# One core, GFNet filter and gated FFN: DRAM scratch stored by sides, filters copied inside SBUF, a new order of the first weight loads, filler matmuls from a built-in constant

## The chip, the core and the metric

The kernel runs on one core of a Trainium2 chip. The core has five engines with instruction queues of their own: TensorE (PE; its weight loads are shown as PEld), VectorE (DVE), ScalarE (ACT), GpSimd (POOL) and SyncE (SP), which here issues every DMA. Each engine runs its queue in order; semaphores tie the queues together. TensorE writes to PSUM, from which DVE and ACT read; all else lives in SBUF with its 128 partitions, or in DRAM. Sixteen DMA engines move the data. The metric is the device time of one launch in microseconds (us), as the median of several runs.

## The reference

```python
x = A_x                                   # [1, 2048, 640] bf16
xn = _layernorm(x, axis=-1)
X = rfft2(xn); X = X * (A_w_r + 1j * A_w_i); s = irfft2(X)     # filter [2048, 321], bf16
g = silu((gelu(xn @ w_gate) * (xn @ w_up)) @ w_down)           # 640 -> 1536 -> 640
return x + s * g
```

A spectral filter (a 2-D real Fourier transform over 2048 rows and 640 columns, a product with a complex filter, and the way back) and a gated feed-forward network read the same normalised input; their product is added to `x`.

## The kernel before

**Slabs.** Row n of `x` is written as n = 16 n2 + n1. `X` holds it as [128 partitions (n2), 16 slabs (n1), 640]. A slab is normalised by `stats` (two `half_stats` of 320 columns on DVE, L174, and their aggregate, L179), `root` (DVE adds the epsilon, POOL raises to the power -1/2, L190) and `norm` (DVE, L196), or by `norm_act` on ACT.

**FFN.** Four slabs make a group g of 512 columns. `slab_T` transposes a normalised slab into `xnT[g]`, on TensorE with the identity or by a DMA transpose; `slab_Tparts` does it for slabs 0 and 1 in two parts (L773, L774). `ffn_piece(g, t, k, c0, c1_)` makes one tile t of 128 of the 1536 hidden units, for gate (k = 0, `Wg`) or up (k = 1, `Wu`), on the columns c0 to c1_: five matmuls over 640 inputs (L714). The gate goes through Gelu on ACT into `ge`, three buffers (L718); the up half is multiplied by it on DVE into `uT` (L720). PSUM has two banks each for gate and up (`psA`, tags g and u), so an up piece needs the DVE product of the up piece two before it. `down_third` does the third matmul (L738), with Silu or Tanh (L743, L746, L747).

**The start.** Group 0 can't wait for four slabs. `ffn_slab(j, tk)` makes pieces of 128 columns for slab j alone. The first three entries of the list `back` do this for slabs 0 and 1 and tiles 0 to 2, with the statistics and norms of slabs 1 to 3 between them; `GG` and `REST` name the pieces. Then come pieces of 256 columns: tiles 3 to 7 on the first half of the group (h0), tiles 0 to 7 on the second (h1). All the rest of group 0 and groups 1 to 3 use 512 columns.

**Filler matmuls.** `warm_pe(n)` issues n matmuls of 256 columns whose result nobody reads (L520): 19 at the very start and two after slab 0's transposes. Both operands are `ones`, which DVE sets by a memset (L202).

**Filter.** The transforms are matmuls with matrices made in the kernel: `slab_S1` (L484) over n2, `group_D` over the columns for a group of one or three slabs (`d_group`, L494 and L498), evacuated by ACT or DVE into `zd` (L510). Then 16 slabs must be combined, for which data must cross partitions: `group_D` stores `zd` to the DRAM scratch `ZDR` (L512), and `load_B2` reads it back as `B2` with another partition meaning (L530). `s2_in` multiplies with `MG` (L556), copies on ACT (L564) and multiplies with both filters `W1` and `W2` on DVE (L568); `s2_out` goes back with `N1`, `N2` (L583), copies on ACT (L589) and stores to `UDR` (L592). This runs in eleven bursts, two for three of 16 filter rows each and one for the last row. `load_V` reads `UDR` as `V` (L603); `gather` (L613), `slab_S1i` (L631), `group_Di`, `group_cs` and `group_Y` do the way back, and `finish` multiplies with the FFN's result, adds `x` and stores.

**Filters in SBUF.** `w_rows` loads `A_w_r` into `W1` and `A_w_i` into `W2`. Partition p = 64 hh + 4 k1 + 2 ri + pm holds rows for k1 with sign pm; both ri hold the same. Each call loads 16 partitions (every fourth) for both `lo`, 16 rows of 321 each, in reverse order for pm = 1 (L118, L120, L121, L123). Rows are padded to LP = 322 elements. `w_edge` halves the first and the last column on POOL (L127).

**Order.** The program is written in order by hand: `back` is the list of FFN steps, and `put(s, ...)` hangs other work behind step s. Each engine's queue follows that order. Every DMA of the kernel stands in SP's one queue, and the DMAs use eight completion semaphores in turn, so a DMA also waits until the one eight places before it has landed.

Of the kernel before, what the change touches and what calls it, by code (L numbers as in the profile page):

```python
# [14 lines left out]
P = 128  # L15
S = 2048
D = 640
L = 321
# [13 lines left out]
def kernel(  # L32
# [28 lines left out]
    ZDR = dram.tile([2, NS, P, L], BF16)  # L61
    UDR = dram.tile([2, NS, P, L], BF16)
# [6 lines left out]
    W1 = wts.tile([P, 2, NS, LP], BF16)  # L69
    W2 = wts.tile([P, 2, NS, LP], BF16)  # L70
# [6 lines left out]
def build(nc, env):  # L77
# [17 lines left out]
    load_w(0, 0, 3)  # L95
    load_x(1, 1)
    load_w(1, 0, 1)
    load_w(1, 1, 3)
    load_x(2, 2)
    load_gu(3, 5)  # L100
    load_gu(5, 7)
    load_gu(7, 8)
# [9 lines left out]
    def w_rows(i, hh, ri, pm):  # L112
        WT, sp = spw[i]
        p0 = hh * 64 + ri * 2 + pm
        for lo in range(2):
            u0 = lo * 32 + hh * 16
            if pm == 0:
                nc.sync.dma_start(out=WT[p0:p0 + 61:4, lo, :, 0:L], in_=sp[:, u0:u0 + 16, :])  # L118
            elif u0 == 0:
                nc.sync.dma_start(out=WT[p0:p0 + 61:4, lo, 1:NS, 0:L], in_=sp[:, 127:112:-1, :])  # L120
                nc.sync.dma_start(out=WT[p0:p0 + 61:4, lo, 0, 0:L], in_=sp[:, 64, :])  # L121
            else:
                nc.sync.dma_start(out=WT[p0:p0 + 61:4, lo, :, 0:L], in_=sp[:, 128 - u0:112 - u0:-1, :])  # L123
# [77 lines left out]
    ones = gtile([256], BF16)  # L201
    nc.vector.memset(ones, 1.0)  # L202
# [30 lines left out]
    def affine(name, src, a, b):  # L233
# [4 lines left out]
    u_f, hi_f, s_f, h_f, pf, n1_f, z_f = bits(  # L238
        "pb", [(0, 63), (6, 1), (0, 31), (5, 1), (0, 127), (1, 15), (0, 1)])
# [14 lines left out]
    u64 = fma("u64", e64, 64.0, u_f)  # L254
# [48 lines left out]
    root(0, 1)  # L303
    inv_consts()
# [199 lines left out]
    def group_D(i):  # L504
        n0, n = DF[i]
        pd = d_group([Zt.pop(n0 + a) for a in range(n)], FT, LH)
        zd = zdbuf[:, i % 2, 0:n]
        for b in range(2):
            ev = nc.vector.tensor_copy if i in (2, 5) and b == 1 else nc.scalar.copy
            ev(out=zd.rearrange("p a c (m b) -> p a c m b", b=2)[:, :, :, :, b], in_=pd[b])  # L510
        for a in range(n):
            nc.sync.dma_start(out=ZDR[:, n0 + a].rearrange("c p l -> p c l"), in_=zd[:, a, :, 0:L])  # L512

    warm_bank = []

    def warm_pe(n):
        if not warm_bank:
            warm_bank.append(bank(0))
        for _ in range(n):
            nc.tensor.matmul(warm_bank[0][:, 0:256], lhsT=ones[:, 0:P], rhs=ones, start=True, stop=True)  # L520
# [3 lines left out]
    def load_B2():  # L524
        B2 = big.tile([P, NH, L], BF16, tag="sB", name="B2")
        zv = ZDR.rearrange("c n (z a k h) l -> a (c n z) k h l", z=2, a=2, k=2)
# [43 lines left out]

    uv = UDR.rearrange("c n (z a k h) l -> a (c n z) k h l", z=2, a=2, k=2)

    def s2_out(b):
# [16 lines left out]
        if l0 + w == L:  # L590
            for lo in range(2):
                nc.sync.dma_start(out=uv[lo][:, :, h0:h0 + n, :], in_=us[64 * lo:64 * lo + 64, :, :, :])  # L592
# [162 lines left out]
    GG, REST = ((0, 0), (1, 0)), ((0, 1), (2, 0))  # L755
# [39 lines left out]
    def put(s, *item):  # L795
        plan[s].append(item)
# [70 lines left out]
    for k in range(16):  # L867
        put(8 + k if k < 8 else (32, 35, 38, 41, 44, 44, 47, 47)[k - 8], w_rows, k // 8, k % 8 // 4, k % 2, k % 4 // 2)
# [32 lines left out]
    warm_pe(19)  # L901
# [44 lines left out]
```

## Time and profile before

| | |
|---|---|
| median of 3 runs | 204.1 us (203.77 to 204.25) |
| profiled execution | 204.42 us, of it 202.6 us from first to last instruction (the span) |
| granted TensorE clock | 1.000 |
| chain that ended last | PE 90%, DVE 4%, DMA 2%, issue 1%, POOL 1% |
| DMA | 31.77 MB in 43315 packets; 41504 of them under 2 KB |
| PE busy by fortieths of the span | 7899999999999999999999999999999999999993 |
| DMA busy by fortieths of the span | 5999999899799999729995233569501334224211 |

A digit is the busy share of one fortieth (5.1 us) in tenths, 9 for 90% or more. "Busy" of PE counts a matmul from its start to its modelled end, and matmuls overlap, so a stretch of nines is not proof of full rate. In rows of the DMA view, the last number is the time from the issue on SP to the landing.

Times of single transfers are from the same execution. The loads at the start, with their issue and landing:

| transfer | KB | issued | landed |
|---|---|---|---|
| X slab 0 | 160 | 0.72 | 3.06 |
| Wg tiles 0-2 | 480 | 1.16 | 5.48 |
| X slab 1 | 160 | 1.63 | 5.99 |
| Wu tile 0 | 160 | 2.19 | 6.69 |
| Wu tiles 1-2 | 320 | 2.66 | 7.80 |
| X slabs 2-3 | 320 | 3.23 | 8.65 |
| Wg tiles 3-4 | 320 | 4.06 | 9.80 |
| Wu tiles 3-4 | 320 | 4.54 | 10.93 |

And around the scratch: the last three stores to `ZDR` were issued at 83.81, 84.21 and 84.72 and landed at 86.74, 88.07 and 88.92. The ten loads of `B2` were issued from 89.00 on, 0.65 apart; the first four landed at 92.72, 93.91, 95.03 and 96.20. The last store to `UDR` landed at 131.97; the loads of `V` were issued from 132.10 on and the first five landed at 134.48, 135.17, 136.15, 138.13 and 139.12. The first copy of `gather` ran at 136.45, the one for slabs 2 and 3 at 138.28.

### The profile page before, as it was taken

Reading aid. Unit: us, or ns where it says so; the run is one execution under the profiler, and the core shown is the slowest. Engines: PE = TensorE matmul, PEld = TensorE weight load, DVE = VectorE, ACT = ScalarE, POOL = GpSimd, SP = SyncE. Lnnn points to the kernel's source line nnn. Section 1 sums busy time; section 2 is a strip of 40 time slices with the busy share of each in tenths; the row PEclk is TensorE's granted clock in tenths of the full one; section 3 lists DMA queues with packets and bytes.
Section 4 is the critical chain, followed back from the end, with each engine's and each line's share of the span. In section 5 each row is a group of like instructions: output and inputs, shape, how many; then the busy total and the mean of one; then the engine's idle time right before and its main releaser. Section 6 shows DMA issues by size and latency. Waiting matters only on the chain.

```text
span 202.6 us, 4209 instructions
## 1 busy us (share of the span) xinstructions
PE 195.6 (97%) x1574; PEld 119.8 (59%) x1589; DVE 129.3 (64%) x340; ACT 122.4 (60%) x208; POOL 33.4 (16%) x61
## 2 busy tenths in 40 slices
PE   7899999999999999999999999999999999999993
PEld 5688854777555555566644333457775555556762
DVE  7886966786488982533576465342358776867672
ACT  2448657857886768423788688425375647476631
POOL 5327779953000200100000000000000000000000
PEclk9999999999999999999999999999999999999999
DMA  5999999899799999729995233569501334224211
GB/s 167 306 297 305 372 310 142 158 147 137 153 170 143 173 174 174 180 43 226 213 228 111 44 97 101 130 164 317 172 0 68 97 102 127 69 92 144 86 69 60
DMA packets 43315, 31.77 MB, mean 157 GB/s; under 512 B 12192, under 2 KB 41504, under 8 KB 43296
## 3 DMA queue, kind: packets, MB, share of 16 engines
q1 hardware_dynamic: 43296, 31.52, 71.4%
q8 instruction: 12, 0.20, 0.4%
q14 instruction: 7, 0.06, 0.1%
HBM read 21.66 MB, written 7.88 MB: 146 GB/s over the span
## 4 chain that ended last, share of the span: by engine, by line
PE 90%; DVE 4%; DMA 2%; issue 1%; POOL 1%; SPq 0%; ACT 0%; DVEq 0%
PE psu L714 25%; PE psg L714 24%; PE psg L738 13%; PE psu L738 12%; PE pd L494 5%; PE pz L484 2%; PE pv L631 2%; PE pu L583 2%; DMA X<-in_A_x_dram 2%; PE px L556 2%; PE pd L498 2%; DVE st L174 1%; DVE uT L720 1%; POOL rst L190 1%; PE pt L326 0%
## 5 line engine op out<-in xcount | busy, mean ns | idle before, releaser
L714 PE MATMUL psu<-xnT,Wu 128*128 128x512 bf16 (+2 forms) x289 | 60.9, 339 | 0.6 <-issue 0.2
L714 PE MATMUL psg<-xnT,Wg 128*128 128x512 bf16 (+2 forms) x286 | 60.4, 338 | 0.9 <-issue 0.5
L720 DVE TENSOR_TENSOR uT<-psu,ge 128x512 bf16<-128x512 f32 (+2 forms) x59 | 34.3, 585 | 29.8 <-PE psu L714 22.5
L718 ACT ACTIVATE ge<-psg 128x512 bf16<-128x512 f32 (+2 forms) x59 | 30.5, 518 | 27.6 <-PE psg L714 25.9
L738 PEld LDWEIGHTS <-uT 128*128 128x128 bf16 x384 | 36.3, 98 | 14.6 <-issue 0.6
L714 PEld LDWEIGHTS <-Wu 128*128 128x128 bf16 x295 | 26.6, 98 | 22.9 <-issue 2.7
L714 PEld LDWEIGHTS <-Wg 128*128 128x128 bf16 x295 | 26.6, 98 | 21.9 <-issue 1.5
L738 PE MATMUL psg<-Wd,uT 128*128 128x320 bf16 (+1 forms) x192 | 30.3, 302 | 0.0
L738 PE MATMUL psu<-Wd,uT 128*128 128x320 bf16 (+1 forms) x192 | 29.2, 296 | 0.0
L568 DVE TENSOR_TENSOR X<-xs,W 128x972 bf16<-128x972 bf16 (+2 forms) x22 | 13.3, 646 | 10.6 <-ACT xs L564 10.6
L174 DVE BATCH_NORM_STATS2 st<-X 128x6 f32<-128x320 bf16 x32 | 14.2, 482 | 0.5 <-DMA X<-in_A_x_dram 0.3
L633 ACT CAST W<-pv 128x640 bf16<-128x640 f32 x16 | 11.1, 692 | 5.4 <-PE pv L631 5.4
L510 ACT CAST GEN<-pd 128x966 bf16<-128x966 f32 (+1 forms) x10 | 10.4, 1102 | 5.3 <-PE pd L498 5.3
L656 ACT ACTIVATE W<-pd 128x960 bf16<-128x960 f32 (+2 forms) x14 | 10.1, 780 | 5.0 <-PE pd L498 5.0
L486 ACT CAST GEN<-pz 128x640 bf16<-128x640 f32 x16 | 11.0, 697 | 3.2 <-PE pz L484 3.2
L589 ACT CAST X<-pu 128x486 bf16<-128x486 f32 (+4 forms) x22 | 12.3, 558 | 0.3
L564 ACT CAST xs<-px 128x972 bf16<-128x972 f32 (+2 forms) x11 | 10.3, 936 | 2.4 <-PE px L556 2.4
L190 POOL TENSOR_TENSOR rst<-ve,mhalf 128x1 f32<-128x1 f32 (+2 forms) x9 | 6.5, 717 | 29.5 <-DVE ve L188 29.5
L662 DVE TENSOR_TENSOR W<-W 128x960 bf16<-128x960 bf16 (+1 forms) x12 | 6.8, 599 | 4.8 <-ACT W L656 4.8
L689 DVE TENSOR_TENSOR Yall<-Yall,G 128x640 bf16<-128x640 bf16 (+3 forms) x18 | 8.1, 450 | 2.1 <-ACT G L743 1.9
L747 DVE SCALAR_TENSOR_TENSOR G<-th,psu 128x320 bf16<-128x320 f32 x8 | 3.9, 488 | 8.4 <-ACT th L746 8.4
L452 DVE TENSOR_TENSOR f<-uvt 128x512 bf16<-128x512 bf16 x16 | 6.7, 421 | 3.0 <-PE pz L484 2.9
(137 smaller groups left out, 202.5 us busy)
## 6 DMA issues: line engine op xcount, KB each, us to landing
ZDR<-GEN SPq DMA_DIRECT2D x16, 160.5 KB, 5.3
xt<-in_A_x_dram SPq DMA_DIRECT2D x8, 320.0 KB, 3.5
UDR<-X SPq DMA_DIRECT2D x10, 240.8 KB, 3.6
W<-in_A_w_r_dram SPq DMA_DIRECT2D x14, 160.5 KB, 7.7
W<-in_A_w_i_dram SPq DMA_DIRECT2D x14, 160.5 KB, 6.0
out_dram<-Yall SPq DMA_DIRECT2D x14, 160.0 KB, 1.8
B<-ZDR SPq DMA_DIRECT2D x8, 240.8 KB, 5.5
Vin<-UDR SPq DMA_DIRECT2D x6, 321.0 KB, 6.3
```

What stands on the lines that cost most here:

```text
L174: nc.vector.bn_stats(out=st[:, k, :], in_=X[:, n1, 320 * k:320 * k + 320])
L486: nc.scalar.copy(out=Zt[n1], in_=pz)
L494: nc.tensor.matmul(out[a][g], lhsT=lhs[a][:, g, :], rhs=T[:, g, 0:w], start=(a == 0), stop=False)
L510: ev(out=zd.rearrange("p a c (m b) -> p a c m b", b=2)[:, :, :, :, b], in_=pd[b])
L564: nc.scalar.copy(out=xs, in_=px[:, :, 0:n * w].rearrange("p k (h l) -> p k h l", l=w))
L568: nc.vector.tensor_tensor(out=pp[-1], in0=xs, in1=WT[:, :, h0:h0 + n, l0:l0 + w], op=ALU.mult)
L589: nc.scalar.copy(out=us[:, :, :, c0:c0 + (w + 1 - m) // 2], in_=pv[:, :, :, m:w:2])
L633: nc.scalar.copy(out=vs, in_=pv)
L714: nc.tensor.matmul(ps, lhsT=WT[:, c, t * P:(t + 1) * P], rhs=xnT[g][:, c, c0:c1_], start=(c == 0), stop=(c == 4))
L718: nc.scalar.activation(out=ges[t], in_=ps, func=ACT.Gelu_apprx_tanh)
L720: nc.vector.tensor_tensor(out=uT[g][:, t, c0:c1_], in0=ps, in1=ges[t], op=ALU.mult)
L738: nc.tensor.matmul(ph, lhsT=uT[g][:, t, j * P:(j + 1) * P], rhs=Wd[:, t, c0:c1_], start=(t == 0), stop=(t == NT - 1))
```

## The change

Four things change.

1. *Scratch by sides.* `ZDR` and `UDR` get an outer axis a, the parity of the partition that wrote (or will read) the row, and the row index within a side runs to 64. The constant `u64` from which `Tinv` and `Tfwd` are made changes with it, so that the same numbers come out at the permuted partitions. `group_D` stores from every second partition: four stores per group of three slabs (two for the single slab) instead of one per slab. `load_B2` and the `UDR` stores now move all 128 partitions for one half of the filter rows (hh), where they moved 64 partitions for both; their number and bytes stay. `load_V` has 20 loads into every second partition instead of 10 into all.
2. *Filters copied in SBUF.* Only the partitions with ri = 0 are loaded from DRAM, nine loads for each filter instead of 18; those with pm = 0 in runs of 16 rows at once, for which the padding of the rows goes (L for LP). `w_twin` then copies them to ri = 1 from SBUF to SBUF, two copies for each filter.
3. *Start.* The first gate load has tiles 0 and 1, and all loads now have two tiles. Slabs 0 and 1 alone are used on tiles 0 to 3 instead of 0 to 2, in the order gate, gate, up, up; the pieces of 256 columns on h0 begin at tile 4. An empty step keeps the numbering of the later steps.
4. *Filler matmuls.* `ones` becomes a constant that the framework sets on POOL ahead of the program; 20 filler matmuls instead of 19 stand first in PE's queue, and two more, whose moving operand is a copy of slab 0's variance, behind them.

```diff
-    ZDR = dram.tile([2, NS, P, L], BF16)
-    UDR = dram.tile([2, NS, P, L], BF16)
+    ZDR = dram.tile([2, 2, NS, 64, L], BF16)
+    UDR = dram.tile([2, 2, NS, 64, L], BF16)
...
-    W1 = wts.tile([P, 2, NS, LP], BF16)
-    W2 = wts.tile([P, 2, NS, LP], BF16)
+    W1 = wts.tile([P, 2, NS, L], BF16)
+    W2 = wts.tile([P, 2, NS, L], BF16)
...
     load_x(0, 1)
-    load_w(0, 0, 3)
+    load_w(0, 0, 2)
     load_x(1, 1)
-    load_w(1, 0, 1)
-    load_w(1, 1, 3)
+    load_w(1, 0, 2)
+    load_gu(2, 4)
     load_x(2, 2)
-    load_gu(3, 5)
-    load_gu(5, 7)
-    load_gu(7, 8)
+    load_gu(4, 6)
+    load_gu(6, 8)
     load_x(4, 4)
...
+    def w_plus(i, hh, lo):
+        WT, sp = spw[i]
+        p0 = hh * 64
+        u0 = lo * 32 + hh * 16
+        nc.sync.dma_start(out=WT[p0:p0 + 61:4, lo].rearrange("p h l -> p (h l)"),
+                          in_=sp[:, u0:u0 + NS, :].rearrange("k h l -> k (h l)"))
+
+    def w_minus(i, hh, lo):
+        WT, sp = spw[i]
+        p0 = hh * 64 + 1
+        u0 = lo * 32 + hh * 16
+        if u0 == 0:
+            nc.sync.dma_start(out=WT[p0:p0 + 61:4, lo, 1:NS, :], in_=sp[:, 127:112:-1, :])
+            nc.sync.dma_start(out=WT[p0:p0 + 61:4, lo, 0, :], in_=sp[:, 64, :])
+        else:
+            nc.sync.dma_start(out=WT[p0:p0 + 61:4, lo, :, :], in_=sp[:, 128 - u0:112 - u0:-1, :])
+
+    def w_twin(i, pm):
+        v = spw[i][0].rearrange("p a h l -> p (a h l)")
+        nc.sync.dma_start(out=v[2 + pm:P:4], in_=v[pm:P:4])
...
-    ones = gtile([256], BF16)
-    nc.vector.memset(ones, 1.0)
+    ones = nc.const_aps.tensor(1.0, (P, 256), BF16)
+    warm_bank = []
+
+    def warm_pe(n, rhs=ones):
...
+            nc.tensor.matmul(warm_bank[0][:, 0:256], lhsT=ones[:, 0:P], rhs=rhs, start=True, stop=True)
+
+    warm_pe(20)
...
-    u64 = fma("u64", e64, 64.0, u_f)
+    u64 = fma("u64", e64, 64.0, fma("u_f", z_f, 32.0, kh_f))
...
     root(0, 1)
+    wv = consts.tile([P, 1], BF16, name="wv")
+    nc.vector.tensor_copy(out=wv, in_=mva[0][:, 0, 1:2])
+    warm_pe(2, wv.to_broadcast([P, 256]))
     inv_consts()
...
-        for a in range(n):
-            nc.sync.dma_start(out=ZDR[:, n0 + a].rearrange("c p l -> p c l"), in_=zd[:, a, :, 0:L])
+        for a in range(2):
+            if n == 1:
+                nc.sync.dma_start(out=ZDR[a, :, n0].rearrange("c p l -> p c l"), in_=zd[a:P:2, 0, :, 0:L])
+            else:
+                for c in range(2):
+                    nc.sync.dma_start(out=ZDR[a, c, n0:n0 + n].rearrange("n p l -> p n l"),
+                                      in_=zd[a:P:2, :, c, 0:L])
...
-            for lo in range(2):
-                nc.sync.dma_start(out=B4[64 * lo:64 * lo + 64, :, h0:h1, :], in_=zv[lo][:, :, h0:h1, :])
+            for hh in range(2):
+                nc.sync.dma_start(out=B4[:, hh, h0:h1, :], in_=zv[:, hh, h0:h1, :])
...
-            for lo in range(2):
-                nc.sync.dma_start(out=uv[lo][:, :, h0:h0 + n, :], in_=us[64 * lo:64 * lo + 64, :, :, :])
+            for hh in range(2):
+                nc.sync.dma_start(out=uv[:, hh, h0:h0 + n, :], in_=us[:, hh, :, :])
...
             for c in range(2):
-                nc.sync.dma_start(out=V[:, n0:n0 + n, c * L:c * L + L],
-                                  in_=UDR[c].rearrange("n p l -> p n l")[:, n0:n0 + n, :])
+                for a in range(2):
+                    nc.sync.dma_start(out=V[a:P:2, n0:n0 + n, c * L:c * L + L],
+                                      in_=UDR[a, c, n0:n0 + n].rearrange("n p l -> p n l"))
...
-    GG, REST = ((0, 0), (1, 0)), ((0, 1), (2, 0))
+    Q = [((t, 0), (t + 1, 0), (t, 1), (t + 1, 1)) for t in (0, 2)]
...
-    back = [(run, (ffn_slab, 0, GG), (norm_parts, 1), (vt_iota, 1), (ffn_slab, 0, REST), (slab_Tparts, 1),
-             (ffn_slab, 0, ((1, 1), (2, 1))),
-             (half_stats, 2, 0)),
-            (run, (ffn_slab, 1, GG + REST[:1]), (half_stats, 2, 1), (root, 2, 1), (ffn_slab, 1, REST[1:])),
-            (run, (ffn_slab, 1, ((1, 1), (2, 1))), (norm, 2), (stats, 3), (root, 3, 1))]
+    back = [(run, (ffn_slab, 0, Q[0]), (norm_parts, 1), (vt_iota, 1), (ffn_slab, 0, Q[1][0:2]), (slab_Tparts, 1),
+             (ffn_slab, 0, Q[1][2:4]), (half_stats, 2, 0)),
+            (run, (ffn_slab, 1, Q[0][0:3]), (half_stats, 2, 1), (root, 2, 1), (ffn_slab, 1, Q[0][3:4] + Q[1][0:1])),
+            (run, (ffn_slab, 1, Q[1][1:4]), (norm, 2), (stats, 3), (root, 3, 1))]
     for h in range(2):
-        for t in range(0 if h else 3, NP):
+        for t in range(0 if h else 4, NP):
             back.append((ffn_part, 0, t, h))
+    back.insert(3, (run,))
...
-    for k in range(16):
-        put(8 + k if k < 8 else (32, 35, 38, 41, 44, 44, 47, 47)[k - 8], w_rows, k // 8, k % 8 // 4, k % 2, k % 4 // 2)
+    WL = [(hh, lo) for lo in range(2) for hh in range(2)]
+    for i, places in enumerate(((8, 9, 10, 11, 12, 13, 14, 15, 26, 27), (32, 32, 35, 35, 38, 38, 41, 41, 47, 48))):
+        for k in range(4):
+            put(places[2 * k], w_minus, i, *WL[k])
+            put(places[2 * k + 1], w_plus, i, *WL[k ^ 1])
+        for pm in range(2):
+            put(places[8 + pm], w_twin, i, pm)
...
-    warm_pe(19)
     norm_parts(0)
```

More of the change, by code (lines that the diff above doesn't have):

```diff
@@ L110, in build @@
     spw = [(WT, src.rearrange("(k1 r) l -> k1 r l", k1=NS)) for WT, src in ((W1, A_w_r), (W2, A_w_i))]
-    def w_rows(i, hh, ri, pm):
+    def w_plus(i, hh, lo):
         WT, sp = spw[i]
-        p0 = hh * 64 + ri * 2 + pm
-        for lo in range(2):
[L116 to L123, printed above, removed]
+        p0 = hh * 64
[14 more added lines that the diff above has]
+        nc.sync.dma_start(out=v[2 + pm:P:4], in_=v[pm:P:4])
     def w_edge(i):
@@ L199, in norm @@
             done.add(("n", n1))
-    ones = gtile([256], BF16)
-    nc.vector.memset(ones, 1.0)
+    ones = nc.const_aps.tensor(1.0, (P, 256), BF16)
+    warm_bank = []
+    def warm_pe(n, rhs=ones):
+        if not warm_bank:
+            warm_bank.append(psA.tile([P, 512], FP32, tag="g", name="psg"))
+        for _ in range(n):
+            nc.tensor.matmul(warm_bank[0][:, 0:256], lhsT=ones[:, 0:P], rhs=rhs, start=True, stop=True)
+    warm_pe(20)
     negpi = c1("negpi")
@@ L236, in affine @@
         return t
-    u_f, hi_f, s_f, h_f, pf, n1_f, z_f = bits(
-        "pb", [(0, 63), (6, 1), (0, 31), (5, 1), (0, 127), (1, 15), (0, 1)])
+    kh_f, hi_f, s_f, h_f, pf, n1_f, z_f = bits(
+        "pb", [(1, 31), (6, 1), (0, 31), (5, 1), (0, 127), (1, 15), (0, 1)])
     cs_f = h_f
@@ L510, in group_D @@
             ev(out=zd.rearrange("p a c (m b) -> p a c m b", b=2)[:, :, :, :, b], in_=pd[b])
-        for a in range(n):
-            nc.sync.dma_start(out=ZDR[:, n0 + a].rearrange("c p l -> p c l"), in_=zd[:, a, :, 0:L])
[L514 to L520, printed above, removed]
+        for a in range(2):
[5 more added lines that the diff above has]
+                                      in_=zd[a:P:2, :, c, 0:L])
     st_b = {}
@@ L525, in load_B2 @@
         B2 = big.tile([P, NH, L], BF16, tag="sB", name="B2")
-        zv = ZDR.rearrange("c n (z a k h) l -> a (c n z) k h l", z=2, a=2, k=2)
+        zv = ZDR.rearrange("a c n (z k h) l -> (a c n z) k h l", z=2, k=2)
         B4 = B2.rearrange("p (k h) l -> p k h l", k=2)
         for h0, h1 in ((0, 3), (3, 6), (6, 9), (9, 12), (12, 16)):
-            for lo in range(2):
-                nc.sync.dma_start(out=B4[64 * lo:64 * lo + 64, :, h0:h1, :], in_=zv[lo][:, :, h0:h1, :])
+            for hh in range(2):
+                nc.sync.dma_start(out=B4[:, hh, h0:h1, :], in_=zv[:, hh, h0:h1, :])
         st_b["B2"] = B2
@@ L569, in s2_in @@
         st_b[b] = pp
-    uv = UDR.rearrange("c n (z a k h) l -> a (c n z) k h l", z=2, a=2, k=2)
+    uv = UDR.rearrange("a c n (z k h) l -> (a c n z) k h l", z=2, k=2)
     def s2_out(b):
@@ L590, in s2_out @@
         if l0 + w == L:
-            for lo in range(2):
-                nc.sync.dma_start(out=uv[lo][:, :, h0:h0 + n, :], in_=us[64 * lo:64 * lo + 64, :, :, :])
+            for hh in range(2):
+                nc.sync.dma_start(out=uv[:, hh, h0:h0 + n, :], in_=us[:, hh, :, :])
     st_c = {}
```

## The prediction

> **What bounds the kernel.** I read the page's busy shares first, then sums by stretch, then the chain of waits at the start, and last the rows of the places that the change touches.
>
> ```profile
> PE 195.6 (97%) x1574; PEld 119.8 (59%) x1589; DVE 129.3 (64%) x340; ACT 122.4 (60%) x208; POOL 33.4 (16%) x61
> ```
>
> ```profile
> 0.00:5.00 5.00, 3.83 (x19) 2.70 (x19) 3.86 (x40) 1.49 (x2) 2.55 (x10) 1.00 0.54 165
> 5.00:15.00 10.00, 8.90 (x106) 7.21 (x105) 8.28 (x32) 4.86 (x14) 2.73 (x5) 1.00 1.17 303
> 15.00:94.00 79.00, 78.42 (x642) 51.00 (x646) 52.40 (x139) 51.61 (x84) 28.16 (x47) 1.00 1.01 188
> 94.00:132.00 38.00, 37.68 (x283) 17.16 (x287) 21.91 (x37) 28.00 (x48) 0.00 (x0) 1.00 0.65 136
> ```
>
> Columns of the second view: stretch, its length, then busy us of PE, PEld, DVE, ACT, POOL, granted clock, DMA share, GB/s. From 15 us on TensorE is busy without a break that matters; a change that removes no matmul can gain only before 15 us, or where PE waits for the scratch in DRAM. The same DMA engines are full up to 94 us, but nothing waits for them there. The chain at the start (start us, us, what):
>
> ```profile
> 1.63 4.36 DMA X<-in_A_x_dram
> ...
> 6.01 0.90 DVE st L174 x2
> ...
> 7.41 0.58 POOL rst L190
> ...
> 8.01 0.39 DVE X L196
> ...
> 8.45 0.56 PE pt L773 x5
> ...
> 12.73 0.81 DVE st L174 x2
> ...
> 13.89 0.44 DVE uT L720
> ...
> 14.37 0.71 PE psu L714 x5
> ```
>
> PE runs out of slab 0's pieces at 7.66 (last start 7.60) and stands 0.79 us until slab 1 is normalised; it stands 0.23 at 11.89 and 0.30 at 14.37, both for a PSUM bank that DVE (L720) has still to read. That is 1.32 us between the first gate matmul (6.44) and full work. Full work needs 0.056 us per 128-column matmul (five to a piece: 0.28) and 0.109 per 256-column one.
>
> The scratch: PE's second half of the first filter burst, and the load that it waits for.
>
> ```profile
> 93.95 0.10 PEld L556 LDWEIGHTS <-MG 64*64 64x64 bf16 x1 [0.30 <-issue]
> B<-ZDR SPq DMA_DIRECT2D x1, 240.8 KB, 4.2
> ```
>
> The second line is the second B load alone: issued at 89.69, landed 4.2 us later, at 93.91. PE could have gone on at about 93.72, so this wait is worth 0.23 us.
>
> **The sum, step by step.** All in the profiled execution's time (span 202.6, 204.42 in all); the median of the runs is 204.1, so I take the difference off the median.
>
> *Filler matmuls.* The 19 start at 1.17, behind DVE's memset of `ones` (0.27 us, L202), 0.21 us each. Afterwards they need no memset and can start near 0.75, when the other engines do (ACT at 0.72); 20 end at about 5.0 and two more, which wait for a DVE copy behind slab 0's variance (about 4.45), at about 5.45. The transposes behind them on PE start at 5.53 in any case: DVE's norm is ready then. Gain 0; loss 0.1 if the copy, 0.06 us of DVE time, pushes the norm at 5.09 (DVE is idle 0.15 before it, which covers it). DVE loses the memset and gains one small operation; X's slab 0 lands at 3.06 and sets the rest. The 256-column filler costs 0.21 up to 4.99 and 0.11 from 5.91, so PE's slow state ends between; starting earlier can only help this, by an amount no row shows: 0 taken, 0.2 as bound.
>
> *Load order.* Landings follow each other by the time that each takes: 1.13 us per 320 KB of gate or up tiles (9.80 to 10.93), 0.51 per 160 KB of X, 1.44 for 480 KB (3 x 128 columns: 640 packets of 768 bytes, 40 per DMA engine, at the 36 ns that the trace gives one). So Wg 0-1 lands at 5.48 - 1.44 + 1.13 = 5.17, X slab 1 at 5.68 (5.99 before), Wu 0-1 at 6.81, Wg 2-3 at 7.94, Wu 2-3 at 9.07, X slabs 2-3 at 9.92 (8.65 before).
>
> *Slab 0 on four tiles.* First gate at 6.44 as before; four pieces end at 7.66 as before. Pieces g2, g3 wait for Wg 2-3: 7.97 to 8.53, 0.31 lost. DVE: slab 1's stats start at 5.73, when the norm of slab 0 is done, 0.28 earlier; but the two products u0, u1 (0.29 each) now stand ahead of slab 1's norm in its queue. Stats, root and constants end at 7.63, the products at 8.2, so the norm starts 0.16 later than the 8.01 of before and the transposes come at about 8.6 (0.05 lost). They end at 8.95; u2, u3 wait for Wu 2-3 until 9.10. Slab 1 starts at 9.66 against 9.39, with two more pieces (0.56) done: 0.29 ahead. Then the third wait: u3 of slab 1 needs the bank of u1, whose product stands behind X 2-3's half statistics (0.49, 0.21, 0.15 on DVE); I get 0.59 there against 0.23, and none where 14.37 was, because four 256-column pieces (2.2 us) now cover slab 3's statistics (1.25). Lost in all: about 0.31 + 0.05 + 0.05 + 0.59 = 1.0 against 1.32. Gain 0.3. Bounds: all waits gone, 1.3; weights 0.5 us later than this, 0.25 lost. The piece count and columns are the same otherwise; ACT and DVE have two more small operations each (0.28), on queues with room.
>
> *Filters.* Each of W1, W2: 18 loads before, now 9 loads and two SBUF copies of 642 KB. The old 160 KB loads landed 1.1 us apart. W1 had landed at 48.9, was scaled on POOL at 50.3, and nothing stands behind that there until 65.4; W2 landed at 83.4, and both are first used at 95.4. Cover of 12 us or more; the copies must wait for their loads and stand in SP's queue ahead of ZDR stores and transposes, whose data come later (49.9, 76.9). Cost 0. If a copy took 10 us, ZDR's last group (83.8) would sit behind it.
>
> *W's row pitch* goes from 322 to 321, so every other row starts off a 4-byte word. Rows:
>
> ```profile
> L720 DVE TENSOR_TENSOR uT<-psu,ge 128x256 bf16<-128x256 f32 x6 | 2.4, 416 | 1.6 <-PE psu L714 0.8 <-ACT ge L718 0.8
> L720 DVE TENSOR_TENSOR uT<-psu,ge 128x128 bf16<-128x128 f32 x6 | 1.6, 288 | 0.1
> L568 DVE TENSOR_TENSOR X<-xs,W 128x972 bf16<-128x972 bf16 x8 | 5.0, 662 | 4.7 <-ACT xs L564 4.7
> L568 DVE TENSOR_TENSOR X<-xs,W 128x642 bf16<-128x642 bf16 x2 | 0.9, 496 | 0.9 <-ACT xs L564 0.9
> L613 DVE COPY vr<-Vin x10: 185/221/222, 136.5 to 172.0; 128x256 bf16<-128x256 bf16 x6, 128x128 bf16<-128x128 bf16 x4
> ```
>
> L720 reads float32: (416 - 288) / 128 = 1.0 ns per element. L568: (662 - 496) / 330 = 0.50, two at a time. If the odd pitch took that away, 972 elements would take about 0.49 us more, twice per burst. The nearest row is L613: its first copy of a pair reads runs that start at element 289, its second at even places, and both forms show one duration (221, 222 at 256 elements). So 0 taken. The Trainium skill, Advanced Engine Details and Errata, section "VectorE Performance Modes", asks for a start on 4 bytes in this mode; by it the total would be that of the second rival. The Trainium skill's Vector Engine (DVE) Microarchitecture Reference, section 5.1, says that alignment made no difference when measured, and by that it stays at the sum below; L613 agrees with the latter, though with one source only.
>
> *Scratch by sides.* The last ZDR group goes out in four stores instead of three: same packets, one issue more (0.45 to 0.5). In the trace's packet records its data is through by 86.9 and the last landing is at 88.92: the landing is not set by the issue. I take the same 5.1 us from data to landing, and 0.5 more as bound. B's loads of 240.8 KB land 1.16 us apart while they fill 64 partitions; the V loads, 128 partitions, 321 KB, 1.05 apart. By V's rate a B load takes 0.79, and the first pair lands 0.37 + 0.37 = 0.74 earlier relative to the first issue. With PE 0.3 earlier, the wait of 0.23 goes: gain 0.2 (0 if B keeps its rate).
>
> *V* is fetched by 20 loads instead of 10, 0.45 each: slabs 0-1 land some 3.6 us after the first issue against 3.07; their first use is 4.35 after it. Covered by 0.7. Slabs 2-3 about 5.8 after against 6.03. Cost 0, bound 0.5.
>
> Sum: 0.3 + 0.2 = 0.5 us; 204.42 becomes 203.9, the median **203.6**.
>
> **Rivals.** (1) *The start gains more*: slab 1's waits vanish, or the filler makes PE fast earlier: up to 1.1 in all, 203.0 to 203.3. For it: the chain shows DVE, not DMA, in most of its steps. Against: 1600 KB must land before u2. (2) *Off the 4-byte word*, slower: L568 at one element at a time in every burst. The second L568 of a burst ends at 102.27 and PE wants it at 102.82: 0.55 of room against 0.98 more, so it decides from 0.27 per operation on. PE then loses 0.4 in every second or in every one of ten bursts: 2 to 4.5 us, 205.6 to 208. Against: L613. (3) *More and smaller transfers are late*: ZDR's fourth store and B at its old rate put the first B pair at 94.1, 0.2 later than now, and weights 0.5 late at the start cost 0.25: 204.3 to 204.7. (4) *Nothing moves*: tile 2-3 weights eat the start's gain, B's wait stays: 204.0 to 204.1.
>
> **How the numbers follow.** Forecast 0.42, rivals 0.22, 0.10, 0.14, 0.12. A measurement of this kernel tells 0.2%, 0.41 us, from no change. The forecast sits just beyond it; two thirds of its share count as faster (0.28), with rival 1 that makes 0.50; same 0.14 + 0.12 = 0.26; slower 0.24. Range 203.0 to 204.9: rival 2 and a tail of rival 1 are left out.
>
> **What would show it.** Right: a PE gap of about 0.3 before g2 and none of 0.8 before slab 1's transposes; tile 0 of the second half of columns (17.68 now) at about 17.4; no wait at the first L556; L568 at 0.66. Wrong: L568 near 1.1; a wait at L556 longer than 0.3; a PE gap before L631's first slabs; a first gate matmul later than 6.44.

## The result and the profile after

The changed kernel takes 237.81 us as the median of 4 runs (237.51 to 238.67); the kernel before took 203.94 in the same session (203.63 to 204.25). The ratio is 1.167, 95% interval 1.163 to 1.171: 16.7% slower, where 0.2% faster was forecast. The profiled execution took 237.51 us, its span is 235.3 (before: 202.6), so 32.7 us have to be found in the trace.

The page of the changed kernel: busy us and share of the span, then PE and its granted clock in tenths, by fortieths of the span (5.9 us each).

```profile
PE 203.0 (86%) x1587; PEld 123.4 (52%) x1602; DVE 129.9 (55%) x342; ACT 122.2 (52%) x209; POOL 33.3 (14%) x61
...
PE   8899999989395929399999999991299999999994
...
PEclk9999999999889988979999999997589999999999
```

PE has lost its row of nines. Counted from 0, there are holes in slices 10, 12, 14 and 16 and a wide one in 27 and 28, and behind most of them the clock is down. PE's busy time itself has grown by 7.4 us although the work is the same but for a few fillers. The sums by stretch, in the columns used before, show how much and where:

```profile
5.00:15.00 10.00, 8.36 (x110) 6.83 (x109) 7.48 (x32) 4.54 (x14) 2.26 (x4) 1.00 1.11 309
15.00:50.00 35.00, 34.95 (x283) 25.32 (x283) 25.83 (x75) 22.67 (x43) 25.03 (x43) 1.00 0.81 234
50.00:116.00 66.00, 49.94 (x369) 29.09 (x372) 27.93 (x71) 29.25 (x43) 3.55 (x5) 0.92 0.38 106
116.00:154.00 38.00, 37.68 (x283) 17.11 (x285) 22.11 (x37) 27.83 (x47) 0.00 (x0) 1.00 0.43 126
154.00:170.00 16.00, 6.24 (x38) 3.61 (x38) 2.28 (x7) 1.94 (x4) 0.00 (x0) 0.75 0.77 204
```

PE is idle for 16 of 66 us in the stretch in which `zd` is stored, and for almost 10 of 16 where `V` comes back; the bursts between them (116 to 154) are as full as before. Both holes have a name in the list of waits (engine, line, releaser: us in total, times, longest):

```profile
ACT GEN L504 <- DMA ZDR<-GEN: 21.1, 5, 5.7
...
PE pz L502 <- ACT GEN L504: 15.6, 5, 4.3
...
DVE vr L629 <- DMA xt<-in_A_x_dram: 10.9, 1, 10.9
...
PE pv L647 <- DVE vr L629: 9.7, 1, 9.7
```

The list before had neither; the row of that copy, L486 there, was the following one.

```profile
ACT GEN L486 <- PE pz L484: 3.2, 6, 0.7
```

L504 (before: L486) is ACT's copy of `pz` into `zbuf`. It now waits for *stores* that read `zd`, which is another region of the same tile `GEN`; before, the same copy waited only for PE. The program's own list of semaphore waits, which is there without a run, says the same (second occurrence of the copy, before and after; five of the 16 copies have such waits now, none had them before):

```
GEN<-pz 128x640 [waits PE]
GEN<-pz 128x640 [waits DMAHW3, DMAHW2, PE]
```

The second wait is the first copy of `gather`. The list names a load of `xt`, because that shares its completion semaphore with a load of `V`; the program waits there on all eight DMA semaphores, that is, for all 20 loads of `V`; before, the first copy waited on two. The timeline of the changed kernel around it (start, us, engine, what, idle before):

```profile
156.02 9.81 SPq L619 DMA_DIRECT2D Vin<-UDR  x15
...
159.22 0.39 PE L647 MATMUL pv<-Tinv,Vin 128*128 128x128 bf16 x4
...
168.96 0.30 DVE L629 COPY vr<-Vin 128x128 bf16<-128x128 bf16 x2 [10.94 <-DMA xt<-in_A_x_dram]
...
169.31 0.29 PE L647 MATMUL pv<-Tinv,vr 128*128 128x128 bf16 x1 [9.70 <-DVE vr L629]
```

Slabs 0 and 1 had landed at 157.41; PE did four of slab 0's five matmuls with them at 159.22. The fifth needs `vr`, and that copy ran 0.4 behind the twentieth landing (168.57).

The rest is the clock. After one of the stalls, from 62.91 on, five 512-column matmuls took 2.34 us; undisturbed they take 1.24. The granted clock (the third column from the end) in the 3.6 us behind the stalls of 4.14, 2.80, 4.42, 4.07 and 9.88 us follows in this order. These lengths are counted from where the last matmul would end at full rate; the profile's idle times of PE (3.97, 2.64, 4.25, 3.90, 9.70) count from its modelled end, about 0.17 us later.

```profile
62.60:66.20 3.60, 3.57 (x19) 2.19 (x19) 1.49 (x3) 2.26 (x4) 0.00 (x0) 0.54 1.03 220
74.60:78.20 3.60, 3.41 (x37) 2.20 (x38) 2.92 (x9) 2.31 (x4) 0.86 (x1) 1.00 0.24 77
86.70:90.30 3.60, 3.57 (x18) 2.20 (x18) 1.63 (x5) 2.25 (x4) 0.46 (x1) 0.53 0.23 94
99.95:103.55 3.60, 3.58 (x21) 2.36 (x21) 0.69 (x1) 1.65 (x3) 0.00 (x0) 0.57 0.00 0
169.30:172.90 3.60, 3.59 (x17) 2.22 (x18) 1.04 (x4) 1.13 (x2) 0.00 (x0) 0.61 0.14 52
```

Four of the five cost a second time: 3.6 x (0.46 + 0.47 + 0.43 + 0.39) = 6.3 us. In all 15.6 + 9.7 + 6.3 = 31.6 of the 32.7 us. Most of the rest is the start: the first `pz` came at 44.24, before at 43.56. The chain of waits there (start, us, what) now has a weight load in it where it had DVE:

```profile
3.24 6.58 DMA Wu<-in_B_w_up_dram
9.82 0.05 issue
9.87 0.73 PE psu L730 x10
```

What had been priced at nothing for the engines did cost nothing. The product with the filters kept its two elements at a time on rows of 321 (form, count, busy, mean ns; before 662 and 496):

```profile
L583 DVE TENSOR_TENSOR X<-xs,W 128x972 bf16<-128x972 bf16 x10 | 6.2, 665 | 5.1 <-ACT xs L579 5.1
...
L583 DVE TENSOR_TENSOR X<-xs,W 128x642 bf16<-128x642 bf16 x2 | 0.9, 495 | 0.9 <-ACT xs L579 0.9
```

### The profile page after: what moved, and what is told of

Read it like the earlier page. It is cut to its first block, busy times and chain, and to the rows that moved or that the text cites. A ratio compares the mean times of both kernels' runs of the same rounds, so it can differ in the third digit from the quotient of the medians.

```text
span 235.3 us, 4254 instructions
## 1 busy us (share of the span) xinstructions
PE 203.0 (86%) x1587; PEld 123.4 (52%) x1602; DVE 129.9 (55%) x342; ACT 122.2 (52%) x209; POOL 33.3 (14%) x61
## 4 chain that ended last, share of the span: by engine, by line
PE 70%; DMA 11%; SPq 10%; ACT 5%; issue 2%; DVE 1%; ACTq 0%
PE psu L730 18%; PE psg L730 18%; PE psg L754 10%; PE psu L754 10%; DMA ZDR<-GEN 7%; SPq L619 5%; PE pd L512 5%; SPq L534 3%; DMA Wu<-in_B_w_up_dram 3%; ACT GEN L528 2%; PE pv L647 2%; PE pu L598 2%; PE pd L516 2%; PE px L571 2%; ACT GEN L504 1%
## 5 line engine op out<-in xcount | busy, mean ns | idle before, releaser
L730 PE MATMUL psg<-xnT,Wg 128*128 128x512 bf16 (+2 forms) x291 | 62.3, 344 | 1.3 <-issue 0.5
L730 PE MATMUL psu<-xnT,Wu 128*128 128x512 bf16 (+2 forms) x294 | 61.8, 339 | 1.2 <-DVE uT L736 0.4
L754 PEld LDWEIGHTS <-uT 128*128 128x128 bf16 x384 | 36.8, 99 | 15.4 <-issue 0.6
L730 PEld LDWEIGHTS <-Wg 128*128 128x128 bf16 x300 | 27.1, 99 | 23.3 <-issue 3.1
L754 PE MATMUL psu<-Wd,uT 128*128 128x320 bf16 (+1 forms) x192 | 30.3, 303 | 0.0
L504 ACT CAST GEN<-pz 128x640 bf16<-128x640 f32 x16 | 10.7, 703 | 21.8 <-DMA ZDR<-GEN 21.1
L502 PE MATMUL pz<-Tfwd,f 128*128 128x128 bf16 x80 | 7.3, 224 | 15.6 <-ACT GEN L504 15.6
L649 ACT CAST W<-pv 128x640 bf16<-128x640 f32 x16 | 11.1, 692 | 15.6 <-PE pv L647 15.6
L583 DVE TENSOR_TENSOR X<-xs,W 128x972 bf16<-128x972 bf16 (+2 forms) x22 | 13.3, 648 | 10.2 <-ACT xs L579 10.2
L502 PEld LDWEIGHTS <-f 128*128 128x128 bf16 x80 | 5.9, 99 | 19.5 <-issue 16.9
L647 PE MATMUL pv<-Tinv,vr 128*128 128x128 bf16 x16 | 3.6, 223 | 9.7 <-DVE vr L629 9.7
```

The lines of the kernel that those rows point to most:

```text
L502: nc.tensor.matmul(pz[:, c, :], lhsT=chunk(f, n1 % 2, c), rhs=Tfwd[:, n1, :], start=True, stop=True)
L504: nc.scalar.copy(out=Zt[n1], in_=pz)
L583: nc.vector.tensor_tensor(out=pp[-1], in0=xs, in1=WT[:, :, h0:h0 + n, l0:l0 + w], op=ALU.mult)
L730: nc.tensor.matmul(ps, lhsT=WT[:, c, t * P:(t + 1) * P], rhs=xnT[g][:, c, c0:c1_], start=(c == 0), stop=(c == 4))
L754: nc.tensor.matmul(ph, lhsT=uT[g][:, t, j * P:(j + 1) * P], rhs=Wd[:, t, c0:c1_], start=(t == 0), stop=(t == NT - 1))
```

## The experiments

All times are medians in us; the ratio is to runs of the kernel before on the same chip in the same session. That kernel's median was 203.68 to 203.94 in the different sessions, so a difference between kernels of two sessions is uncertain by some 0.3 us.

| kernel | us | before | ratio (95%) |
|---|---|---|---|
| own_z | 217.34 | 203.68 | 1.067 (1.064 to 1.070) |
| own_v | 224.31 | 203.68 | 1.100 (1.098 to 1.103) |
| own_zv | 205.03 | 203.68 | 1.0070 (1.0049 to 1.0092) |
| old_scr | 204.32 | 203.68 | 1.0025 (1.0010 to 1.0039) |
| b_start | 204.45 | 203.73 | 1.0037 (1.0023 to 1.0051) |
| b_fill | 203.74 | 203.73 | 0.9998 (0.9990 to 1.0007) |
| sides_own | 205.17 | 203.73 | 1.0072 (1.0053 to 1.0090) |
| sides_half | 203.96 | 203.73 | 1.0011 (1.0002 to 1.0020) |
| own_zd | 203.94 | 203.77 | 1.0005 (0.9991 to 1.0019) |
| halves | 204.12 | 203.77 | 1.0015 (1.0001 to 1.0029) |
| half_fill | 204.19 | 203.77 | 1.0018 (1.0004 to 1.0032) |
| b_filters | 204.32 | 203.77 | 1.0024 (1.0009 to 1.0040) |
| start_late | 204.72 | 203.89 | 1.0042 (1.0026 to 1.0059) |
| start_swap | 204.51 | 203.89 | 1.0031 (1.0020 to 1.0043) |
| start_split | 203.91 | 203.89 | 1.0004 (0.9994 to 1.0013) |

### Are the waits real needs or only side effects of shared tiles?

**own_z** gives `zbuf` a tile of its own:

```diff
-    zbuf = fv.rearrange(...).bitcast(BF16)[:, 0:4 * D].rearrange(...)
+    zbuf = big.tile([P, 4, 5, P], BF16, tag="zb", name="zbuf")
```

> Kernel: the changed kernel with the transform's buffer zbuf (which ACT fills from pz, L504) in a tile of its own instead of a region of GEN; all transfers stay as they are. Theory A (the five stalls of 0.95, 4.14, 2.80, 4.42 and 4.07 us before pz are a wait that only exists because zd, which the ZDR stores read from every second partition, and zbuf lie in one tile): the stalls go, 16.4 us, and with four of the five long ones the stretches of about 3.4 us after them in which 512-column matmuls ran at 427 ns instead of 216, about 1.5 us each. 237.8 - 16.4 - 6 = about 215.4; the wait of 9.9 us at the first L647 stays. Rival B (the strided stores themselves are too slow, and the wait only shows it): the wait moves to the scratch's way back, with PE waiting at the first L571 or L528 behind the stores, and less than half is won, over 225. Rival C (the slow matmuls are not an effect of the stalls): stalls go, PE busy stays at 202 or more, about 221.

Measured: 20.5 us of the loss went, the stalls at L504 with it; PE's busy time fell to 200.1, so with only the stall of 9.9 us left some of the slow matmuls left too, which speaks against rival C. It is 2 us short of theory A. Part of that is in this list of waits of own_z:

```profile
ACT GEN L528 <- DMA ZDR<-GEN: 6.2, 3, 2.3
...
PE pz L502 <- ACT GEN L528: 0.4, 1, 0.4
```

The wait has moved to the evictions into `zd`: the two halves of `zd` lie in one tile as well, and an eviction into one half now waits for the stores that read the other.

**own_v** leaves that as it was and gives the first two pieces of `V` tiles of their own.

```diff
+            V = big.tile([P, n, 2 * L], BF16, tag=f"sV{n0}", ...) if n0 < 4 else Vall[:, n0:n0 + n, :]
```

> Kernel: the changed kernel with the first two pieces of V (slabs 0 and 1, slabs 2 and 3) in tiles of their own; the 20 strided loads stay. Theory A (the first gather waited for all 20 loads, the last of which landed at 168.57, though its own four had landed by 157.41): first copy of gather 0.2 to 0.4 us behind the fourth landing, the stall of 9.9 us goes and one cold stretch of about 1.5 us, 237.8 - 11.4 = about 226.4. The wait of the third piece for the last load remains, up to 0.5 us. Rival B (the loads themselves come too late for PE): PE waits at L647 for several us in all, at the third and later pieces, over 230. Five stalls before pz as before, 16 us.

Measured: 13.5 us went, two more than expected; the stall at L647 is gone, and five stalls before `pz` stay. By the list they come to 13.7 us here against 15.6 in the changed kernel, which is about the two that were not expected. In this profile a stall of 3.11 us was followed by a clock of 0.50 and one of 2.62 by 1.00.

**own_zv** has both edits, own_z's and own_v's.

> Kernel: both of these together: zbuf in two tiles of its own whose place the first two pieces of V take later; every transfer of the changed kernel stays as it is. Theory A: all of the loss but that of the start goes: 203.9 of the kernel before + 0.7 (start) + 0 to 0.4 (third piece of V) - 0 to 0.2 (second half of the first burst) = 204.4 to 205.0, PE busy 195 to 197. Rival B (stores and loads by every second partition are slow themselves): 206 or more, PE waiting at L571, L528 or L647. Rival C (slow matmuls for another reason than the stalls): PE busy 202, 211 or more.

Measured: 205.03, theory A's upper end; rivals B and C, with 206 and 211 or more, fall. 32.8 of 33.9 us are back with every stepped transfer still in place, and PE is busy 196.5.

**sides_own, sides_half, own_zd** have the old start and old fillers, to be free of the start's scatter, and the copied filters. sides_own has own_zv's tiles. sides_half leaves all in the shared tiles but makes a side a half of the partitions; the constants of `Tinv` are permuted to match:

```diff
-                    ... in_=zd[a:P:2, :, c, 0:L])
+                    ... in_=zd[64 * a:64 * a + 64, :, c, 0:L])
...
-                    nc.sync.dma_start(out=V[a:P:2, n0:n0 + n, ...
+                    nc.sync.dma_start(out=V[64 * a:64 * a + 64, n0:n0 + n, ...
```

own_zd keeps the stepping and `zbuf` in `GEN`, but gives each half of `zd` a tile, besides own_v's:

```diff
+    zdbuf = [big.tile([P, 3, 2, LP], BF16, tag=f"sV{k}", name=f"zd{k}") for k in (0, 2)]
```

> Kernel: scratch by sides, with zbuf and the first two pieces of V in tiles of their own, and the filters copied in SBUF, on the old start and the old filler matmuls. Theory: PE needs 2.84 us from the first px to the first pu where it needed 3.28 with the old scratch, the same from there on, and the filters cost nothing: 203.7 - 0.4 = 203.3. Rival: the 20 loads of V or the stores cost it back, or the filters cost: 203.7 or more.

> Kernel: the same as sides_own in its parts, but the sides are the halves of the partitions instead of every second one (Tinv's constants permuted for it), so that no store or load steps over partitions, and zbuf and V stay in the shared tiles. Theory A (only the stepping makes the shared tiles wait): no stall before pz, none at the first L647 over 0.5, 203.3 as with sides_own. Issue of a V load 0.45 us instead of 0.61 to 0.65. Rival (transfers of 64 adjoining partitions are slow, as the old B loads were at 1.16 us for 240.8 KB): the last stores to ZDR land later and the first half of the first burst with them, up to 1 us: 203.7 to 204.3. Rival D (the tile is shared, so it waits in any case): over 225.

> Kernel: as sides_own, but instead of zbuf the two halves of zd lie in tiles of their own (the first two pieces of V take their place later); every store and load still steps over every second partition, and the evictions into zd now wait for the stores of two groups before, no longer for those of the group just before. Theory A (what sides_own lost against sides_half is this last wait of the evictions, 7.6 us on ACT and 0.96 us on PE before pz): 203.9 to 204.2, no PE wait before pz. Rival B (transfers of every second partition are slow in themselves; they took 0.61 to 0.65 us to issue): 205.0 as sides_own.

Measured: sides_own missed by 1.9 us, on the rival's side. Its timeline shows a part of why, an eviction that waits for stores and `pz` behind it:

```profile
76.42 2.33 ACT L519 CAST GEN<-pd 128x966 bf16<-128x966 f32 x2 [1.97 <-DMA ZDR<-GEN]
...
77.70 0.44 PE L493 MATMUL pz<-Tfwd,f 128*128 128x128 bf16 x5 [0.44 <-ACT GEN L519]
```

From the first `pz` to the first `px` its profile took 50.80 us, those of sides_half and own_zd 49.96 and 49.95, as before (49.96). These 0.8 us are most of the 1.2 between their medians. The rest of the 1.9 is in the main the forecast gain itself, which sides_half did not bring either: 203.96 where 203.3 was expected.

sides_half has no such wait, nor any of the two large ones, with the tiles shared: rival D falls. own_zd has none either, with the stepping: its list of waits holds no `ZDR` store at all. The copy of `pz` has the row of the kernel before again in both (first sides_half, then own_zd):

```profile
ACT GEN L494 <- PE pz L492: 3.2, 6, 0.7
...
ACT GEN L493 <- PE pz L491: 3.2, 6, 0.7
```

own_zd's 203.94 is sides_half's 203.96. So the cause is stepping and sharing *together*: a transfer that takes every second partition of a tile is held against the other regions of that tile that these kernels use. The programs' lists of semaphore waits agree: in sides_half and own_zd no copy of `pz` waits for a DMA, and the first copy of `gather` waits on four DMA semaphores instead of eight. Either one alone costs nothing of note. What was also wrong in my expectation of sides_half: its `V` loads took 0.61 us to issue as well, so that price belongs to loads of 64 partitions, and they landed more slowly, the last 19.3 us behind the first issue against 15.9 stepped (own_zd) and 12.9 with 128 partitions (before). The Trainium skill, DMA: Bandwidth & Descriptors, section "Rules for kernel authors", says that transfers to the two halves of the partitions gain nothing by being separate and advises one of 128; 19.3 against 12.9 agrees. PE did not wait for it here.

### What are the other parts worth?

old_scr is the changed kernel with the old scratch, halves the changed kernel with sides as halves; b_start, b_fill and b_filters are the kernel before with one part each; half_fill is the kernel before with sides as halves and the new fillers.

> Kernel: the changed kernel with the scratch as it was before (layout, stores, loads, constants); load order, slab 0 on four tiles, filters copied in SBUF and filler matmuls stay. Theory A: start loses 0.7 us (the fifth half-column tile came at 27.54 against 26.86), the filters cost nothing: 203.9 + 0.7 = 204.6. The forecast on record says that these parts gain 0.3: 203.6. If the filters or the row pitch cost anything, it shows as a wait or a longer L583: 205 or more.

> Kernel: the one before, with the new load order and slab 0 on four tiles alone. Theory S (this part is the loss of the start): the landing of Wu 0-1, which came anywhere from 6.70 to 7.61 in five profiles of the new start, decides; first pz 0.3 to 1.3 us later than in the kernel before, median 204.2 to 204.6 beside 203.7. Rival F (the filler matmuls are the loss): 203.4, the gain of 0.3 on record, here.

> Kernel: the one before, with the new filler matmuls alone. Theory S: 203.7, within 0.2 of the kernel before; first gate matmul at 6.4 to 6.5. Rival F (two more matmuls behind the copy of the variance, or PE's start without the memset, hold back the transposes): 204.1 to 204.4, and the first gate matmul later than 6.5.

> Kernel: the changed kernel whole, with the sides as halves of the partitions instead of every second one, so that no transfer steps over partitions. What is left of its loss is what its other parts do. Theory: no stall before pz or at the first L647; the start scatters with the landing of Wu 0-1 (6.6 to 7.6), B's wait is gone: 203.96 of sides_half + 0.2 to 0.8 = 204.2 to 204.8. Forecast on record for the change: 203.6. Rival (the loss of b_start was B's wait alone, 0.4 to 0.6 between px and pu in its profile): 203.9.

> Kernel: the one before with scratch by sides as halves of the partitions and the new filler matmuls; load order, slabs and filters as before, the constant u64 made behind the first statistics. Theory: px to pu 2.85 us in every run, where the old scratch took 2.85 in one profile and 3.26 to 3.47 in others: 203.5 to 203.7, with less scatter than the kernel before. Rival (the small cost of sides_half, 0.2 us, lies in the scratch): 203.9.

> Kernel: the one before with the filters copied in SBUF and the rows of W1 and W2 without padding. Theory: hidden by more than 12 us, and L568 stays at 0.66 us: 203.7, within 0.2 of the kernel before. Rival (the copies fill the DMA engines when the last stores to ZDR go out): px to pu longer than 3.3 us, 204.1 or more. Rival (off the 4-byte word): 205.6 or more.

Measured: the fillers are worth nothing (b_fill). The new start costs 0.4% in b_start. The filters cost 0.24% alone, where I had expected nothing; their copies made nobody wait in its profile. The rival that they fill the DMA engines at the last `ZDR` stores falls as well: the last copy landed at 77.89, and the first store of the last group was issued at 83.66. The parts do not add up: old_scr, which has the new start and the copied filters, lost 0.25%, and halves, the whole change without stepping, 0.15% (204.12, just under the expected 204.2).

Scratch by sides took 2.84 to 2.88 us from the first `px` to the first `pu` in all twelve profiles that have it; the old scratch took 2.85 in one (b_fill) and 3.25 to 3.47 in the other four (before 3.26). The chain of own_zd has one piece of `px` there, where that of the kernel before had two with a break at 93.91:

```profile
93.46 0.32 PE px L568 x2
93.78 1.79 PE psg L754 x12
```

Yet half_fill missed: 204.19, no faster than before. Its first `pz` is late (43.84; `Wu` 1-2 landed at 8.63, in the other six profiles of the old start at 7.32 to 7.89), and how much of its 0.4 us this explains, one profile doesn't say. b_fill's profile, without that break, is of a run of 203.67; that of the kernel before, with it, is of one of 204.42, and its usual time in these sessions is 203.7 to 203.9. So the wait of 0.23 us that the forecast meant to win back is probably not there in most runs. Where it is there it costs more than 0.23: from first `px` to first `pu`, the kernel before took 0.4 us longer than b_fill, old_scr and b_filters 0.4, b_start 0.6. Why b_start, old_scr and b_filters had it stays open.

### Why does the start not gain?

The ten profiles of the new start, with the landing of two loads, first `pz`, and the distance of the last two:

| kernel | Wu 0-1 | Wg 2-3 | first pz | pz - Wg 2-3 |
|---|---|---|---|---|
| old_scr | 6.70 | 7.77 | 43.16 | 35.39 |
| b_start | 6.55 | 7.79 | 43.33 | 35.54 |
| own_v | 6.88 | 7.97 | 43.44 | 35.47 |
| own_z | 7.12 | 8.20 | 43.71 | 35.51 |
| own_zv | 7.31 | 8.44 | 43.97 | 35.53 |
| halves | 7.59 | 8.72 | 44.23 | 35.51 |
| after | 7.61 | 8.73 | 44.24 | 35.51 |
| start_split | 6.59 (tile 1) | 8.32 | 43.73 | 35.41 |
| start_swap | 5.63 | 8.21 | 43.98 | 35.77 |
| start_late | 7.84 | 6.72 | 44.11 | 37.39 |

The last three are halves with the loads in another order:

```diff
 start_late:  load_x(1, 1); load_w(0, 2, 4); load_w(1, 0, 2); load_w(1, 2, 4)
 start_swap:  load_w(1, 0, 2); load_x(1, 1); load_gu(2, 4)
 start_split: load_x(1, 1); load_w(1, 0, 1); load_w(1, 1, 2); load_gu(2, 4)
```

> Kernel: halves with Wg 2-3 loaded ahead of Wu 0-1; all else as in halves. Theory T (the landing of Wu 0-1 sets the end of the start): it lands about 1.1 us later, 7.7 to 8.7, and the first pz comes 36.6 us behind it, 44.3 to 45.3; median about 204.1 + 1.0 = 205.1. Rival (DVE's chain of statistics and norms sets it, and the landing only goes with it): first pz as in halves, 43.4 to 44.2, median 204.1.

> Kernel: halves with Wu 0-1 loaded ahead of X slab 1. Theory T: Wu 0-1 lands at 5.6 to 6.6 and no longer sets the end; X slab 1 lands at 6.1 to 7.0 instead of 4.9 and slab 1's statistics start up to 1 us later, which PE's eight pieces of slab 0 (2.2 us) and the wait for Wg 2-3 cover but for 0 to 0.5: first pz 43.1 to 43.7, 203.7 to 204.0. Rival (whatever load comes fourth lands late): X slab 1 at 7 or later, first pz over 44, 204.3 or more.

> Kernel: halves with Wu 0-1 as two loads of one tile. Theory T, and the late landing belongs to the 320 KB load: Wu 0 lands at 6.2 to 6.7 as in the old start, u0 waits for nothing, Wu 1 lands 0.5 to 1.0 later; first pz 43.2 to 43.8, 203.9. Rival (the place in the queue makes it late): Wu 1 lands at 7.3 to 7.6 and more, first pz as in halves, 204.1 to 204.4.

Measured: with the order of the change, the first `pz` follows the landings at a fixed distance, over a scatter of 1.1 us. start_swap shows that it isn't `Wu` 0-1 by itself: that landed at 5.63, and PE then stood for `Wg` 2-3 (8.21). Theory T as I put it falls. `Wg` 2-3, the end of the first 1280 KB, fits nine of the ten within 0.4 us, but so does `Wu` 2-3, which lands about 1 us behind it in these nine, and more closely: the first `pz` comes 34.40 to 34.42 us behind `Wu` 2-3 in seven of the ten, and 34.59, 34.67 and 35.21 behind it in b_start, start_swap and start_late. The chain of waits up to 16 us goes through `Wu` 2-3 in after, halves and own_zv, through `Wg` 2-3 in own_v, own_z and start_split, through X slab 1 in start_swap, through `Wu` 0-1 in start_late, and through no weight load in old_scr and b_start, the two earliest. So the late starts are those with late weights of tiles 2 and 3, but that one load alone sets the end is not shown. start_late came out 0.3% slower than halves by their ratios, but its first `pz` in the profile no later, so that run doesn't decide alone. The statistics of slab 1 are not it: X slab 1 lands at 4.67 to 5.20 in the first seven without any order to the first `pz`. Between 4 and 5.5 us the DMA engines are busy to 0.77 to 0.87 in the changed kernel, where they were at 1.08 or more before, though all six first loads were issued by 3.3. What makes them pause is open. start_split is the best of this start and equals the kernel before. No version beat it by more than the measurement can tell.

## Why the prediction was wrong

**The steps that failed are *Scratch by sides* and *V*.** Both priced the transfers (packets, issues, time to land) and asked only whether those who need the data wait longer. They did not ask who else would be made to wait. The first was to gain 0.2; the wait of L504 for the `ZDR` stores, and the cold clock behind it, cost 20.5 us (after to own_z). The second was to cost 0, with 0.5 as bound; the wait of the first `gather` for all 20 loads cost 13.5 (after to own_v). The two add up to 34.0, and removing both together with the third wait (own_zd, which also has the old start and fillers) brings 33.9. The waits stand in the program's own list of semaphores; the forecast rested on the order of the instructions alone, which the change left as it was around L504 and L629.

Their sizes were off as well, and that was harmless: a `V` load took 0.65 us to issue, not 0.45, and slabs 0-1 landed 4.68 us behind the first issue (152.73 to 157.41), not 3.6. The reading side was right: B's second load landed 0.64 behind the first (113.80, 114.44; forecast 0.79, before 1.19), and no wait stood before the second half of the first burst. As said above, though, the 0.2 us to be won there was one execution's wait, and mis-sized in that one: 0.4.

***Load order* and *slab 0 on four tiles*** were to gain 0.3; b_start loses 0.7, most of which its profile has at the scratch (the 0.6 above). The start itself shows in the first `pz`: it came at 43.16 to 44.24, on average 43.73, in the seven profiles with the order of the change, and at 43.23 to 43.84, on average 43.50, in the seven with the old one, so 0.2 later and not 0.3 earlier. The failed term is the landing of the weights of tiles 2 and 3: put at 7.94 (`Wg`) and 9.07 (`Wu`) by adding loads back to back, they came at 7.77 to 8.73 and 8.74 to 9.82. In the changed kernel PE stood 0.55 before g2 where 0.31 was forecast, 0.47 before u0 where none was, and 0.55 before u3 of slab 1 (0.59 forecast); the wait of 0.8 before slab 1's transposes did go. First gate at 6.44 was 6.52.

***Filler matmuls*** at 0: right (b_fill). ***W's row pitch*** at 0: right, L583 at 665 ns; the rule of the Trainium skill's Advanced Engine Details and Errata, section "VectorE Performance Modes", that such a start falls out of the fast mode would have meant 205.6 or more, and no run shows that. ***Filters*** at 0: b_filters measured 0.24%; the cover was there, 0.4 of its 0.55 us are the scratch's wait in its profile, and the cause is open.

**The rivals.** The third named waits for more and smaller transfers whose data come late, at 204.3 to 204.7; the direction was right, the mechanism another. "A PE gap before L631's first slabs" (L647 in the changed kernel) stood in the list of what would prove the forecast wrong, and came, 9.7 us long. The range had no room for a wait between regions that never touch.

## What to carry to other kernels

Where a change gives a transfer another shape on a tile that is shared, compare which instructions wait for which semaphores before and after, for every region of that tile; here two changed slices added 25 us of waits that no data needed, and a tile for each region, or sides that lie together, took them away. Price a PE stall of more than about 2 us with the slow stretch that may follow it; whether it does depends on where the stall falls (next section). A wait of 0.2 us in one profile is not yet a gain to be had: see first whether it is there in most runs.

## What the runs showed of the hardware

Stalls of PE of 0.91, 0.95, 2.62 and 2.80 us left the granted clock at 1.00; those of 3.11, 3.68, 4.07, 4.14, 4.25, 4.42 and twice 9.88 were followed by 3.6 us at 0.50 to 0.64 on average. Within a profile the granted clock changed only at steps of 3.41 us: in the changed kernel it was 0.50 from 62.90 to 66.31, from 86.79 to 90.21, from 100.45 to 103.86 and, three steps long, from 161.89 to 172.13. What fits all 17 profiles is the idle time of PE within the step before. With 2.06 us of it or more a clock of 1.00 fell (own_v, 92.94 to 96.35: PE busy 1.35 of 3.41 us), with up to 1.67 it stayed (after, 230.15 to 233.56: PE busy 1.74). The stalls of 2.62 and 2.80 left it at 1.00 because each was split between two steps (2.80: 1.17 and 1.49 us), which is a matter of where they fell. The Trainium skill, TensorE: Matmul & The Clock Gate, Part 1, has half rate after an idle window of about 3.4 us that runs freely, and full rate after as long a busy one; the steps of 3.41 us agree, but here a step did not have to be idle throughout.

Loads of every second partition were faster than loads of 64 adjoining ones: the last `V` load landed 15.9 us behind the first issue in own_zd against 19.3 in sides_half, and 15.8 to 17.5 in the other five profiles with stepped loads against 19.0 in halves. And the landing of `Wu` 0-1, the fourth load at the start, scattered by 1.1 us (6.55 to 7.61) over seven profiles of the same order.
